# Sliding-window attention and an ELU layer on one core: which engine adds two kept products for a quarter of the output

## The chip, the core and the metric

The kernel runs on one core of a Trainium2 chip. A core has five engines that run their own instruction streams and meet through semaphores: TensorE (PE; its weight loads are listed as PEld), VectorE (DVE), ScalarE (ACT), GpSimd (POOL) and SyncE (SP), which here only issues transfers. The metric is the device time of one execution in microseconds, the median over runs of the same kernel. Lower is better.

## What is computed

The reference is attention with a sliding window and a linear distance bias, followed by two matrix products with an ELU between them:

```python
# q, k, v: (8, 8, 576, 64); w_in: (512, 2048); w_out: (2048, 512)
scores = scale * np.matmul(q, k.transpose(0, 1, 3, 2))
bias = slopes[:, None, None] * (-np.abs(rel))[None, :, :]
mask = (rel >= 0) & (rel < 128)
scores = np.where(mask, scores + bias[None], -1e9)
attn = softmax(scores)
x = np.matmul(attn, v).transpose(0, 2, 1, 3).reshape(4608, 512)
h = x @ w_in
g = np.where(h > 0.0, h, np.exp(np.minimum(h, 0.0)) - 1.0)
out = g @ w_out            # (4608, 512), float32
```

## The kernel before, in words

The 4608 tokens are cut into nine blocks of 512 (NTB = 9), and the attention runs over eight batches of 576 tokens. One hand-written schedule mixes three kinds of work in numbered slots (`s`): the attention of a later batch, the hidden layer of a token block (`hidden` and `elu`, into the tile `g`), and the output product of an earlier block. In each slot the loop at the end of the program issues first the `early` work, then the `hidden` products of the slot, the `elu` of the slot before, the slot's `tasks`, its output products (`OUT`), and the `late` work. The order in which the program calls things is the order in which each engine executes its own.

`hidden` (L305 to L316) multiplies on TensorE into one of the PSUM banks `hp`. ScalarE and GpSimd then make the exponential of the negative part in the SBUF tile `e`, in one of two ways. In slots named SOFT, ScalarE does both steps (L312, L313). In the others, two slots out of every eight, ScalarE takes the exponential (L315) and GpSimd clamps it (L316, called the clamp below). VectorE combines `e` and the bank into `g` (L323) and so frees the bank for a later hidden product.

The output product of most tokens is not computed with eight block products but with seven: for a pair `n` of output tiles (256 tokens, two tiles of 128 rows, `n` from 1 to 17) the 2048 rows of `w_out` and its 512 columns are halved, and sums of quarters are multiplied. Precomputed differences of `w_out` quarters stand in `T` (1 to 4), sums of `g` quarters are made on VectorE by `sums` into `S` (1 to 4, 128x1024 float16 each, L354). `product` (L393) runs the seven products, eight matmuls of 256 columns each, accumulating into two PSUM banks in turn (`op` and `av`). Products 1, 6, 7 and 5 are kept: ScalarE copies the bank into the SBUF tiles `U1`, `U6`, `U7`, `U5` (L396, 128x256 float32, one buffer each). The order of the products is 1, 2, 6, 5, 7, 3, 4, spread over eight slots, seven matmuls in each.

The four quarters of a pair's output are put together in `ob` tiles (three buffers): C11 = U1 + bank and C12 = U6 + bank on VectorE (`add`, L354), the lower left quarter as a plain copy of the bank by ScalarE (L398), and C22, the lower right quarter, as U7 + U5. C22 reads SBUF alone. It is called at the head of the tasks in the slot after the pair's last products, some 5 us after U7 was copied. After C12 and C22 the finished tile is stored by a transfer that SyncE issues (`put`, L412). The SyncE queue also carries the transposes of the attention's result into `xT`.

The last pair (n = 17) has a schedule of its own: all its products stand in two slots, and its C22 waits for the copies of products 5 and 7 shortly before the end.

Other work on VectorE in the same stretch: the multiplication of the exponentials with a table (`EX` by `TAB`, L241, 128x1024 float16, both in SBUF), the normalisation of the attention's result (`xn`, L260 and L277), and transposes of q and k from the staging tile `st` (L145). Other work on GpSimd: it issues the loads of q and k (`load_qk`, L108) and of v (`load_v`, L114), each issue a GpSimd instruction of 0.67 to 0.88 us.

Of the kernel before, what the change touches and what calls it, by code (L numbers as in the profile page):

```python
# [11 lines left out]
ALU = mybir.AluOpType  # L12
# [6 lines left out]
def kernel(  # L19
# [9 lines left out]
    nc = tc.nc  # L29
# [4 lines left out]
    NTB = NTOK // 512  # L34
# [3 lines left out]
    V = nc.vector  # L38
# [41 lines left out]
    op = ps_o.tile([128, 512], F32, name="op", tag="op")  # L80
# [68 lines left out]
    with tc.manual_schedule():  # L149
# [203 lines left out]
        def add(o, a, b, op=ALU.add):  # L353
            V.tensor_tensor(out=o, in0=a, in1=b, op=op)  # L354
# [16 lines left out]
        def place(n, i):  # L371


            z, x = XY[n] if n < 2 * NTB - 1 else (sp[2], sp[3] if i == 2 else sp[0])
            return (z if i in (1, 4, 6, 7) else x)[:, 0:256]

        def kept(n, i):
            if (n, i) not in U:
                U[n, i] = work.tile([128, 256], F32, name=f"U{i}", tag=f"U{i}", bufs=1)
            return U[n, i]  # L380

        def tile_out(n, i):
            if (n, i) not in obs:
                obs[n, i] = work.tile([128, DO], F32, name="ob", tag="ob")
            return obs[n, i]
# [14 lines left out]
        def combine(n, what):  # L400
            if what == "C11":
                add(tile_out(n, 0)[:, 0:256], kept(n, 1), place(n, 2))
            elif what == "C12":
                add(tile_out(n, 0)[:, 256:512], kept(n, 6), place(n, 3))
                put(n, 0, 0, DO)
            else:
                add(tile_out(n, 1)[:, 256:512], kept(n, 7), kept(n, 5))
                put(n, 1, 0 if n < 2 * NTB - 1 else 256, DO)

        def put(n, i, c0, c1, queue=nc.sync):  # L410
            r = 256 * n + 128 * i
            queue.dma_start(out[r:r + 128, c0:c1], tile_out(n, i)[:, c0:c1])  # L412
# [218 lines left out]
        for n in SEVEN:  # L631
            s = 15 + 8 * n
            ps = (19, 20, 21, 22, 23, 25, 27, 29, 30) if n == 1 else range(s, s + 9)
            if n < 2 * NTB - 1:
                for d, i in ((-1, 1), (1, 2), (3, 3), (4, 4)):
                    (at_once if n > 2 else at)(ps[d] if d > 0 else ps[0] - 1, sums, n, i)
                after(ps[2], combine, n, "C11")
                after(ps[6], combine, n, "C12")
                (at_once if n > 2 else at)(ps[8], combine, n, "C22")
                for d in range(8):  # L640
                    OUT[ps[d]] = [(product, (n, i, j, j + 1)) for i, j in turns[7 * d:7 * d + 7]]
            else:
                at_once(s - 3, sums, n, 3)
                for i in (2, 1):
                    at_once(s - 2, sums, n, i, 0, 6)
                    at_once(s - 1, sums, n, i, 6, 8)
                at(s - 1, product, n, 1)
                OUT[s] = [(product, (n, 2)), (combine, (n, "C11")), (sums, (n, 4)), (product, (n, 6)), (product, (n, 5))]
                OUT[s + 1] = [(product, (n, 7)), (product, (n, 3)), (combine, (n, "C22")), (combine, (n, "C12")),
                              (product, (n, 4)), (last_out, (n,))]  # L650
# [48 lines left out]
```

The softmax here doesn't subtract the row's maximum and nothing guards it: scores larger than these inputs give would overflow.

## Time and profile before

Three runs took 310.35, 310.82 and 310.94 us; the median is 310.82. One execution was profiled; its span from the first to the last instruction is 308.9 us.

| What | Value |
|---|---|
| median of three runs | 310.82 us |
| span of the profiled execution | 308.9 us |
| mean granted TensorE clock | 0.998 of full speed |
| VectorE sums U7 + U5 (`ob<-U,U`) | 17, mean 0.415 us, first at 70.3, last at 304.2 us |
| GpSimd clamps (`e<-e`, L316) | 44, median 0.612 us (0.602 to 0.838) |
| VectorE `EX` by `TAB` (L241) | 48, median 0.685 us |
| VectorE `S` sums of full size (L354) | 66, mean 0.68 us |
| stores from `ob` on SyncE | 35, landing after 2.2 us (median) |
| idle time of GpSimd before its clamps, until ScalarE's `e` | 152.9 us |

Busy time of each engine in stretches of the same execution, in us:

| Stretch (us) | PE | DVE | ACT | POOL |
|---|---|---|---|---|
| 70 to 90 | 19.9 | 18.9 | 17.0 | 8.8 |
| 90 to 120 | 29.9 | 27.5 | 25.4 | 10.7 |
| 150 to 180 | 29.9 | 27.3 | 25.2 | 9.9 |
| 240 to 270 | 29.9 | 25.0 | 26.3 | 1.8 |
| 270 to 290 | 20.0 | 15.0 | 15.1 | 1.2 |

In a line of the profile, L305 is line 305 of the program, `out<-in` are the tiles written and read, and the shapes are partitions x elements. In rows of the timeline the first number is the start in us from the beginning of the span, the second the length; a bracket at the end tells how long the engine had been idle and who ended it. A group's line gives total busy us and the mean of one in ns after the first bar, then the engine's idle time just before the group and what ended most of it. Two instructions of one engine can overlap slightly, since the next begins while the last results of the first are written.

### The profile page before, as it was taken

How to read it: one execution, taken by the hardware profiler on the slowest of the kernel's cores; microseconds unless marked ns; L12 is line 12 of the kernel's file. 1: busy time of each engine (PE TensorE's matmuls, PEld its weight loads, DVE VectorE, ACT ScalarE, POOL GpSimd, SP SyncE). 2: the span in 40 equal slices, each digit the busy share in tenths (PEclk: the TensorE clock that was granted, in tenths of full speed). 3: DMA queues.
4: the chain of work that ended last, by engine and by line, in shares of the span. 5: the costliest groups of instructions: out<-in, count | busy, mean ns of one | idle time of the engine just before them, and what ended most of it. 6: DMA issues, size and time to landing. Idle time of an engine off the chain costs nothing.

```text
span 308.9 us, 9820 instructions
## 1 busy us (share of the span) xinstructions
PE 300.1 (97%) x4071; PEld 256.1 (83%) x4071; DVE 257.5 (83%) x498; ACT 241.8 (78%) x446; POOL 108.4 (35%) x163
## 2 busy tenths in 40 slices
PE   6899999999999999999999999999999999999995
PEld 4788875798888888988888888888899888898884
DVE  4646888988989998997989998989998788886782
ACT  4576678678798788878887889778888897968871
POOL 8937867273252315141616061706000001010000
PEclk9999999999999999999999999999999999999999
DMA  9999999999194919395969896999530202030103
GB/s 96 196 197 202 201 180 185 94 118 115 21 165 63 169 35 161 43 152 59 132 70 138 110 102 78 138 124 122 60 94 7 91 17 87 19 98 0 70 28 110
DMA packets 96509, 32.04 MB, mean 104 GB/s; under 512 B 83920, under 2 KB 91984, under 8 KB 96464
## 3 DMA queue, kind: packets, MB, share of 16 engines
q0 software_dynamic: 75920, 18.36, 64.2%
q1 hardware_dynamic: 20400, 12.98, 17.1%
q8 instruction: 32, 0.52, 0.7%
q14 instruction: 13, 0.11, 0.1%
q10 hardware_dynamic: 144, 0.07, 0.1%
HBM read 36.70 MB, written 9.44 MB: 149 GB/s over the span
## 4 chain that ended last, share of the span: by engine, by line
PE 72%; DVE 8%; DMA 6%; ACT 5%; POOL 4%; issue 4%; POOLq 0%; DVEq 0%
PE hp L305 33%; PE op L393 13%; PE av L393 12%; DMA VP<-in_v_dram 4%; PE spa L225 3%; PE spa L271 3%; DVE g L323 3%; POOL e L316 2%; PE sp L393 2%; ACT e L315 2%; DMA s<-in_q_dram 2%; ACT EX L236 1%; PE sp L253 1%; POOL VP L114 1%; DVE xn L260 1%
## 5 line engine op out<-in xcount | busy, mean ns | idle before, releaser
L305 PE MATMUL hp<-xT,wi 128*128 128x256 f16 (+3 forms) x1488 | 144.2, 245 | 1.0 <-DVE g L323 0.5
L305 PEld LDWEIGHTS <-wi 128*128 128x128 f16 x1600 | 119.9, 98 | 18.1 <-issue 6.3
L323 DVE SCALAR_TENSOR_TENSOR g<-e,hp 128x512 f16<-128x512 f32 x138 | 93.7, 679 | 22.2 <-ACT e L313 12.5
L316 POOL TENSOR_SCALAR e<-e 128x512 f32<-128x512 f32 x44 | 28.0, 636 | 158.8 <-ACT e L315 152.9
L312 ACT ACTIVATE e<-hp 128x512 f32<-128x512 f32 x98 | 58.6, 597 | 28.5 <-PE hp L305 23.1
L313 ACT ACTIVATE e<-e 128x512 f32<-128x512 f32 x100 | 63.1, 631 | 3.2
L393 PEld LDWEIGHTS <-S 128*128 128x128 f16 x544 | 51.2, 98 | 6.7 <-issue 0.6
L393 PEld LDWEIGHTS <-g 128*128 128x128 f16 x408 | 38.2, 98 | 4.7 <-issue 0.6
L241 DVE TENSOR_TENSOR EX<-EX,TAB 128x1024 f16<-128x1024 f16 x48 | 32.9, 686 | 6.2 <-ACT EX L236 4.0
L114 POOL DMA_DIRECT2D VP<-in_v_dram x40 | 34.6, 878 | 0.6 <-PE hp L305 0.3
L315 ACT ACTIVATE e<-hp 128x512 f32<-128x512 f32 x40 | 24.1, 601 | 10.9 <-PE hp L305 10.9
L393 PE MATMUL op<-T,S 128*128 128x256 f16 x200 | 30.0, 273 | 0.1
L233 ACT ACTIVATE EX<-spa 128x1024 f16<-128x1024 f32 x24 | 24.6, 1025 | 3.7 <-PE spa L225 3.4
L393 PE MATMUL av<-T,S 128*128 128x256 f16 x176 | 26.4, 273 | 0.1
L236 ACT ACTIVATE EX<-sp 128x512 f16<-128x512 f32 x48 | 26.0, 596 | 0.0
L354 DVE TENSOR_TENSOR S<-g 128x1024 f16<-128x1024 f16 (+2 forms) x35 | 23.5, 671 | 0.8 <-PE op L393 0.2
L393 PE MATMUL op<-wo,g 128*128 128x256 f16 x128 | 19.2, 272 | 0.1
L393 PE MATMUL av<-wo,g 128*128 128x256 f16 x120 | 18.0, 272 | 0.0
L277 DVE TENSOR_TENSOR xn<-spa,rden 128x512 f16<-128x512 f32 x24 | 16.6, 692 | 0.8
L108 POOL DMA_DIRECT2D st<-in_k_dram x24 | 16.2, 686 | 2.8 <-DMA s<-in_q_dram 1.9
L108 POOL DMA_DIRECT2D st<-in_q_dram x24 | 15.9, 666 | 0.6 <-DMA VP<-in_v_dram 0.6
L271 PE MATMUL spa<-VP,EX 128*128 128x65 f16 x336 | 15.4, 193 | 0.1
(139 smaller groups left out, 379.3 us busy)
## 6 DMA issues: line engine op xcount, KB each, us to landing
out_dram<-ob SPq DMA_DIRECT2D x35, 256.0 KB, 2.2
VP<-in_v_dram POOLq DMA_DIRECT2D x32, 128.0 KB, 5.7
st<-in_k_dram POOLq DMA_DIRECT2D x24, 144.0 KB, 5.2
st<-in_q_dram POOLq DMA_DIRECT2D x24, 144.0 KB, 5.9
wi<-in_moe_w_in_dram POOLq DMA_DIRECT2D x4, 512.0 KB, 10.7
wo<-in_moe_w_out_dram POOLq DMA_DIRECT2D x4, 512.0 KB, 10.1
VP<-in_v_dram POOLq DMA_DIRECT2D x8, 64.0 KB, 5.8
s<-in_k_dram POOLq DMA_DIRECT2D x1, 512.0 KB, 12.1
```

The costliest lines, as they stand in the source:

```text
L108: nc.gpsimd.dma_start(st[b][32 * g:32 * g + 32, w, :, :, :, :].rearrange("p h n j d -> p (h n) (j d)"), (q, k)[w][b, 2 * g:2 * g + 2, :, : ...
L114: nc.gpsimd.dma_start(VP[b % 2][0:p, n, :, 0:D], v[b, :, 128 * n:128 * n + p, :].rearrange("h p d -> p h d"))
L236: nc.scalar.activation(unit(b, u)[:, g, :, :], sp[g].rearrange("p (h c) -> p h c", h=2), AF.Exp, scale=0.125)
L241: V.tensor_tensor(out=e, in0=e, in1=TAB[:, int(u == 3), 2 * gp:2 * gp + 2, :, :], op=ALU.mult)
L271: nc.tensor.matmul(a[:, h // 4, h % 4, :], ex_[u][:, c:c + 128], VP[b % 2][:, n, h, 0:D + 1], start=j == 0, stop=j == len(parts) - 1)
L305: nc.tensor.matmul(p[:, l * w + u0:l * w + u1], w_in_sb[:, c, fc * 128:(fc + 1) * 128], xT[:, c, x0:x0 + u1 - u0], start=(c == 0), stop=(c ...
L312: nc.scalar.activation(e[:, 0:n], p[:, 0:n], AF.Relu, scale=-1.0)
L313: nc.scalar.activation(e[:, 0:n], e[:, 0:n], AF.Exp, scale=-1.0)
L315: nc.scalar.activation(e[:, 0:n], p[:, 0:n], AF.Exp)
L316: nc.gpsimd.tensor_scalar(out=e[:, 0:n], in0=e[:, 0:n], scalar1=1.0, scalar2=0.0, op0=ALU.min, op1=ALU.max)
L323: V.scalar_tensor_tensor(out=gs[t][:, f0:f0 + nf, c0:c0 + w], in0=sh(es.pop((t, c0, f0))), scalar=1.0, in1=sh(hps.pop((t, c0, f0))), op0=A ...
L393: nc.tensor.matmul(o, a[:, j, :], b[:, j, :], start=j == 0 and i in (1, 2, 5), stop=j == 7, skip_group_check=True)
```

## The change

For the pairs 1 to 16 the sum U7 + U5 is issued to GpSimd in place of VectorE. Pair 17 keeps VectorE. The inputs, the output tile and the place in the program are the same.

```diff
             else:
-                add(tile_out(n, 1)[:, 256:512], kept(n, 7), kept(n, 5))
+                (V if n == 2 * NTB - 1 else nc.gpsimd).tensor_tensor(
+                    out=tile_out(n, 1)[:, 256:512], in0=kept(n, 7), in1=kept(n, 5), op=ALU.add)
                 put(n, 1, 0 if n < 2 * NTB - 1 else 256, DO)
```

In the instruction streams this takes 16 rows out of VectorE's and puts 16 into GpSimd's. There they stand as follows: one or two load issues after the last clamp of the pair for pairs 1 to 9, directly after the second clamp for pairs 10 to 14, and at the end of the queue for pairs 15 and 16. The order on TensorE, ScalarE and SyncE stays. ScalarE's copy into U5 of the next pair now also waits for GpSimd, and the store of the tile waits for ScalarE and GpSimd in place of ScalarE and VectorE.

## The prediction

> **What bounds the kernel now.** I read the page from the top: busy times, the chain that ended last, then the waits of TensorE, then single rows of the timeline around the sixteen sums that move.
>
> ```profile
> PE 300.1 (97%) x4071; PEld 256.1 (83%) x4071; DVE 257.5 (83%) x498; ACT 241.8 (78%) x446; POOL 108.4 (35%) x163
> ...
> PE 72%; DVE 8%; DMA 6%; ACT 5%; POOL 4%; issue 4%; POOLq 0%; DVEq 0%
> ```
> Two groups of instructions, each shape by itself (columns: line, engine, operation, tiles, shapes and count, then busy us and mean ns of one, then idle time before them and what ended it):
>
> ```profile
> L354 DVE TENSOR_TENSOR ob<-U,U 128x256 f32<-128x256 f32 x17 | 7.1, 415 | 1.9 <-ACT U L396 1.9
> ...
> L316 POOL TENSOR_SCALAR e<-e 128x512 f32<-128x512 f32 x44 | 28.0, 636 | 158.8 <-ACT e L315 152.9 <-issue 5.8
> ```
>
> TensorE (PE) is busy 300.1 of 308.9 us and most of its idle time lies before the first moved sum (70.25 us): over 69 to 300 us it is busy 230.2 of 231. VectorE (DVE) is full as well there, 203.8 of 231 us, but it is the second limit, not the first. The first group is the work that moves: 17 sums of two kept products, 0.415 us each, of which 16 go. The second is the only arithmetic that GpSimd (POOL) does in the steady part.
>
> A busy PE can hide short waits, since a row's modelled end reaches past the start of the next. So I took the starts of the single matmuls: a 256-column one normally follows its predecessor by 0.109 us (8 take 0.87). After 69 us, 26 starts are late by over 0.1 us, 4.4 us in all; before 25 of them a VectorE instruction had ended 0.05 to 0.06 us earlier. That 4.2 us is everything VectorE costs the path, and a ceiling for this change.
>
> **What is removed.** 16 x 0.415 = 6.6 us of VectorE time. It shortens the path only where the sum stands in an unbroken run of VectorE work that ends in a late matmul. I followed each of the 25 back to the first idle gap of VectorE. In 21 the run does not hold the sum: it starts at a wait for ScalarE or GpSimd, mostly a g that waits for its e. In four it does, at two places. The plainer is pair 3, in the VectorE rows and then the PE rows:
>
> ```profile
> 103.37 0.42 DVE L354 TENSOR_TENSOR ob<-U,U 128x256 f32<-128x256 f32 x1
> 103.70 0.17 DVE L259 RECIPROCAL rden<-sp 64x4 f32<-64x4 f32 x1
> ...
> 105.48 0.64 DVE L323 SCALAR_TENSOR_TENSOR g<-e,hp 128x512 f16<-128x512 f32 x1
> 106.05 0.66 DVE L354 TENSOR_TENSOR S<-S,g 128x1024 f16<-128x1024 f16 x1
> 106.65 0.76 DVE L145 STREAM_TRANSPOSE KT<-st 128x576 int32<-128x576 int32 x1
> 107.34 0.64 DVE L323 SCALAR_TENSOR_TENSOR g<-e,hp 128x512 f16<-128x512 f32 x1
> ```
> ```profile
> 106.17 1.03 PE L305 MATMUL hp<-xT,wi 128*128 128x256 f16 x8
> 107.04 0.38 PE L393 MATMUL av<-wo,g 128*128 128x256 f16 x2
> 107.26 0.71 PE L393 MATMUL op<-T,S 128*128 128x256 f16 x5
> 108.03 1.03 PE L305 MATMUL hp<-xT,wi 128*128 128x256 f16 x8
> ```
>
> The hidden products at 106.17 and 108.03 start just after a g has freed their bank, 0.19 and 0.23 us late; a third late start at 110.77 (0.10) ends the same run. Of the first, 0.09 is the change from 32-row to 128-row matmuls, which every such place shows and which stays. That leaves 0.10 + 0.23 + 0.10 = 0.43, and no more than the 0.415 by which the run moves up. Pair 1 gives 0.154 - 0.095 = 0.06 at 71.91. Sum of the gains: 0.47 us.
>
> The other 14 sums leave before a stretch in which VectorE waits for another engine anyway; their 5.8 us become idle time. At the end of the kernel (pair 16, sum at 300.91) the next products wait for PE itself: the S made at 301.58 is first used at 303.58.
>
> **What is added.** Sixteen sums on GpSimd, each 256 + 256 elements read and 256 written per partition. The trace of before has no two-input operation there. Nearest row: the clamp L316, 512 read and 512 written, 0.61 us when nothing disturbs it. Below: half of it, 0.31, if only the 256 outputs count. Above: twice, 1.22, if each input costs a pass of its own and the fixed part too. I take 0.65, near the row with equal reads.
>
> POOL has room: 108.4 us busy. What counts is where the sum stands in its queue. On VectorE it waited its turn, a slot or more after its inputs; on GpSimd it comes behind the second clamp of the pair, or behind one or two DMA issues after that. For pairs 1 to 14 the second kept product is done before then (pair 11: copied by 223.05, clamp over at 225.81), and for 15 and 16 the queue is empty and the sum starts when the copy ends. So nothing urgent waits behind it: the next clamp, which gates a g and so PE, is 11 to 14 us away. Behind the sums of pairs 1 to 10 stand one to five loads of q, k and v, each then some 0.65 us later, for a batch that is used many slots on; they land in 5 to 6 us by the page and nothing on the path waits for one after 70 us. On SP, the store behind the sum and the xT transposes behind that store see the sum at the old time or earlier. The U5 copy of the next pair on ScalarE now waits for GpSimd; it comes over 2 us after the sum (closest for pair 17, 302.91). Extra waits of some 0.02 us on ScalarE and VectorE I put at nothing, since both idle between groups; uncovered they would be 16 x 0.02 = 0.3.
>
> **What it may collide with.** GpSimd and VectorE get in each other's way in this trace: the clamp mostly takes 0.60 to 0.64 us, but the six that began 0.28 to 0.37 us before the end of a VectorE product of two SBUF tiles (EX by TAB) took 0.76 to 0.84. At 98.02 the clamp began while EX ran until 98.30, and ended 0.47 after it.
>
> ```profile
> 97.62 0.68 DVE L241 TENSOR_TENSOR EX<-EX,TAB 128x1024 f16<-128x1024 f16 x1
> ```
> ```profile
> 98.02 0.76 POOL L316 TENSOR_SCALAR e<-e 128x512 f32<-128x512 f32 x1 [8.62 <-ACT e L315]
> ```
>
> No row shows the reverse, a VectorE product that comes while GpSimd computes; by the rows a product could be held for nothing or for the whole sum. Places, from the GpSimd queue: pairs 1, 3, 4, 6, 7 and 8 ask while an S or EX is running and just wait (6 and 7 by only 0.08 and 0.03 us); pairs 2, 9, 14 and 15 meet nothing. In pairs 10 to 13 the sum starts as the clamp ends (225.81) and the next S comes at 226.57, then EX, then the values at 227.92, already late:
>
> ```profile
> 225.84 0.69 DVE L323 SCALAR_TENSOR_TENSOR g<-e,hp 128x512 f16<-128x512 f32 x1 [0.30 <-POOL e L316]
> 226.57 0.69 DVE L354 TENSOR_TENSOR S<-g 128x1024 f16<-128x1024 f16 x1
> 227.18 0.69 DVE L241 TENSOR_TENSOR EX<-EX,TAB 128x1024 f16<-128x1024 f16 x1
> ```
>
> The room is 0.76 us, so 0.65 passes and anything longer pushes PE by the excess. Pair 16's sum (299.95 to 300.60) may hold the S at 300.38 by 0.2, with 0.4 in hand. Pair 5 is the open one: the sum asks at 133.42, S runs until 133.59 and EX stands right behind it. If GpSimd gets in between, EX and the late values at 134.24 lose about 0.65 - 0.14 = 0.5 us (0.14 being the part of a clamp, 0.61 - 0.47, that passes before it is held). Cost 0 or 0.5; I take half, 0.25.
>
> The Trainium skill speaks against the change twice. "SBUF — State Buffer", Who interferes with whom: a VectorE instruction with two SBUF inputs and a GpSimd instruction that reads SBUF lock each other out, and the later one blocks fully. The 0.76 us clamps agree for one direction; no row here shows the other. "GPSIMD Engine Reference", Performance versus the Vector engine: a float32 add of 2048 columns takes 4497 ns; an eighth, 0.56 us, is my estimate from it, and with it the sum below would be about 0.05 us lower. No row here shows it.
>
> **Sum.** -0.47 + 0.25 = -0.2 us. The span would be 308.7; 1.9 us lie between the span of 308.9 and the median of 310.82, so 310.6. (The page gives no other time of the profiled execution.)
>
> **Rivals.**
> - *GpSimd's sum is long, and holds VectorE* (slower). At 1.22 us: S and EX of pairs 10 and 11 come 0.42 late with PE right behind (0.84), pairs 12 and 13 some 0.2 each behind a little slack, and pair 5 1.1. With the gain: -0.47 + 0.84 + 0.4 + 1.1 = +1.9, 312.7. It decides (over +0.6) from about 0.9 us on: 0.8 for pair 5 and 0.15 each for 10 to 12. For it: two operands through an engine that needs 0.61 for 512 elements of one. Against: equal reads in the nearest row, and the 0.415 saved soon after each hold.
> - *VectorE's room reaches PE everywhere* (faster). If a quarter of the 4.2 us of late starts goes, 1.05 us: 309.8. For it: VectorE above 90% from 70 to 120 us. Against: 21 of 25 runs hold no such sum and begin at a wait for ScalarE or GpSimd.
> - *Nothing reaches PE, either way*: 310.8, no different from the forecast by measurement.
>
> **How the numbers follow.** A measurement of this kernel tells no change from one within 0.2%, 0.62 us. The forecast with the third rival (310.2 to 311.4) gets 0.50, the long sum 0.34, the faster case 0.16. The range, 309.9 to 311.9, takes in pair 5 lost outright, sums up to about 1.0 us and some of the faster case.
>
> **What would show it.** The L354 sums on VectorE fall from 17 to 1 and a new GpSimd row of 16 appears at 0.6 to 0.75 us; VectorE busy falls by 6.6; the late starts at 106.17, 108.03 and 110.77 shrink together by 0.4. S after the clamp of pairs 10 to 13 still follows its g by 0.04 us: if it follows later, the rival is at work. EX at pair 5 directly after S, or half a microsecond later, settles that. Wrong makes it a GpSimd row above 0.9 us, or late starts that vanish where VectorE had waited for ScalarE.

## The result: 0.27% slower, and where it went

With the change the kernel takes 311.42 us (median of 16 runs, 310.88 to 313.49), against 310.80 us before (16 runs on the same chip, 309.85 to 311.43). The medians lie 0.62 us, 0.20%, apart. The ratio taken over the single runs, which all comparisons below use too, is 1.0027, with a 95% interval of 1.0016 to 1.0038: slower by 0.27%. That is small, near the 0.2% under which the prediction takes a change for none, but the interval lies above 1 altogether. The profiled execution has a span of 309.6 us, 0.7 us more than before.

The page of the changed kernel, busy times and the chain that ended last:

```profile
PE 300.1 (97%) x4071; PEld 255.9 (83%) x4071; DVE 254.6 (82%) x482; ACT 241.9 (78%) x446; POOL 122.2 (39%) x179
...
PE 75%; DVE 6%; ACT 6%; POOL 4%; DMA 4%; issue 3%; POOLq 0%; DVEq 0%; ACTq 0%
```

TensorE does the same work in the same busy time. VectorE has 16 instructions fewer, GpSimd 16 more. Three groups of the changed kernel, each shape by itself, with the columns of the groups shown before:

```profile
L241 DVE TENSOR_TENSOR EX<-EX,TAB 128x1024 f16<-128x1024 f16 x48 | 33.4, 697 | 7.3 <-ACT EX L236 4.6 <-ACT EX L233 2.6
L354 DVE TENSOR_TENSOR S<-g 128x1024 f16<-128x1024 f16 x33 | 23.7, 719 | 0.7 <-PE op L393 0.2
...
L407 POOL TENSOR_TENSOR ob<-U,U 128x256 f32<-128x256 f32 x16 | 14.2, 888 | 24.0 <-ACT U L396 23.9
```

The last line is the new one, mean 0.888 us. The first two are VectorE products that the change does not touch, and both are longer: S had a mean of 686 ns before (22.6 us in all), EX 686 (32.9). That is 1.1 + 0.5 us of VectorE time, though each of these instructions does the same work. A group mean can't say which ones; rows can. TensorE's waits, the view that names who was waited for, has a line that the kernel before does not have (total us, times, longest):

```profile
PE spa L271 <- DVE EX L241: 1.0, 2, 0.7
```

Two waits of TensorE for an EX, 0.26 and 0.74 us. They belong to pairs 4 and 5. These are the GpSimd (POOL), VectorE and TensorE rows at pair 5:

```profile
132.04 0.69 DVE L323 SCALAR_TENSOR_TENSOR g<-e,hp 128x512 f16<-128x512 f32 x1 [0.32 <-POOL e L316]
132.64 0.66 POOL L108 DMA_DIRECT2D st<-in_q_dram  x1
132.76 0.91 DVE L354 TENSOR_TENSOR S<-g 128x1024 f16<-128x1024 f16 x1
133.31 0.94 POOL L407 TENSOR_TENSOR ob<-U,U 128x256 f32<-128x256 f32 x1
133.60 1.21 DVE L241 TENSOR_TENSOR EX<-EX,TAB 128x1024 f16<-128x1024 f16 x1
...
134.86 0.42 PE L271 MATMUL spa<-VP,EX 128*128 128x65 f16 x8 [0.74 <-DVE EX L241]
```

The same place in the kernel before, where the sum was still on VectorE and came later:

```profile
132.89 0.69 DVE L354 TENSOR_TENSOR S<-g 128x1024 f16<-128x1024 f16 x1
133.50 0.69 DVE L241 TENSOR_TENSOR EX<-EX,TAB 128x1024 f16<-128x1024 f16 x1
...
133.84 0.82 PE L271 MATMUL spa<-VP,EX 128*128 128x65 f16 x16
```

Before, S and EX took 0.69 each here, and the values' product on TensorE ran through without an idle stretch. Now S takes 0.91 and EX 1.21, together 0.74 more, and TensorE stands for 0.74. The sum's row begins at 133.31, EX can begin only when S is through (133.60). EX ends at 134.81, which is 0.56 after the sum's end at 134.25. Pair 4, the same engines:

```profile
116.74 0.99 DVE L354 TENSOR_TENSOR S<-g 128x1024 f16<-128x1024 f16 x1
117.66 0.68 DVE L241 TENSOR_TENSOR EX<-EX,TAB 128x1024 f16<-128x1024 f16 x1
117.75 1.16 POOL L407 TENSOR_TENSOR ob<-U,U 128x256 f32<-128x256 f32 x1
...
118.39 0.42 PE L271 MATMUL spa<-VP,EX 128*128 128x65 f16 x8 [0.26 <-DVE EX L241]
```

Here EX is undisturbed and the sum waits for it (it ends 0.57 after EX). But S took 0.99, 0.30 too long, and it ended at 117.73, before the sum's row begins at 117.75. The row as the profile shows it can't be what held S; four of the experiments below ask what did.

The span also holds the loads at the start, which differ from those of the trace before by up to 0.8 us and once by 1.6. A sharper measure is the time of TensorE between the same two matmuls, from the one at 69.30 (time of the trace before) to the start of the last. It is called the TensorE interval below:

| Stretch (times of the trace before) | before | changed | difference |
|---|---|---|---|
| 69.30 to 110.77 (pairs 1 to 3) | 41.47 | 41.17 | -0.30 |
| 110.77 to 134.24 (pairs 4 and 5) | 23.48 | 24.54 | +1.06 |
| 134.24 to the last matmul | 170.98 | 171.07 | +0.09 |
| TensorE interval | 235.92 | 236.78 | +0.86 |

So there was a small gain where it was expected, and a loss of a microsecond in two pairs.

### The profile page after: what moved, and what is told of

Its sections match the earlier page's. It is cut to its first block, busy times and chain, and to the rows that moved or that the text cites. A ratio compares the mean times of both kernels' runs of the same rounds, so it can differ in the third digit from the quotient of the medians.

```text
span 309.6 us, 9854 instructions
## 1 busy us (share of the span) xinstructions
PE 300.1 (97%) x4071; PEld 255.9 (83%) x4071; DVE 254.6 (82%) x482; ACT 241.9 (78%) x446; POOL 122.2 (39%) x179
## 4 chain that ended last, share of the span: by engine, by line
PE 75%; DVE 6%; ACT 6%; POOL 4%; DMA 4%; issue 3%; POOLq 0%; DVEq 0%; ACTq 0%
PE hp L305 34%; PE op L393 13%; PE av L393 12%; PE spa L225 4%; DMA s<-in_q_dram 3%; PE spa L271 3%; DVE g L323 2%; PE sp L393 2%; ACT e L315 2%; POOL VP L114 2%; PE op L329 1%; POOL e L316 1%; PE sp L253 1%; DVE EX L241 1%; PE sp L305 1%
## 5 line engine op out<-in xcount | busy, mean ns | idle before, releaser
L354 DVE TENSOR_TENSOR S<-g 128x1024 f16<-128x1024 f16 (+2 forms) x35 | 24.8, 708 | 0.8 <-PE op L393 0.2
L407 POOL TENSOR_TENSOR ob<-U,U 128x256 f32<-128x256 f32 x16 | 14.2, 888 | 24.0 <-ACT U L396 23.9
```

## The experiments

Each kernel was timed beside the kernel before on its own chip; the TensorE interval is of its one profiled execution. The last two columns are the late starts of the values' product at pairs 4 and 5 (0.12 and 0.16 us before, 0.42 and 0.90 with the change).

| Run | us | before, us | ratio and interval | TensorE interval | pair 4 | pair 5 |
|---|---|---|---|---|---|---|
| e1_pairs45_on_vector | 310.58 | 310.81 | 0.9989 (0.9972 to 1.0006) | 235.93 | 0.13 | 0.16 |
| e2_only_pairs45 | 312.61 | 310.81 | 1.0048 (1.0030 to 1.0066) | 237.29 | 0.44 | 0.91 |
| e3_right_after_clamp | 310.21 | 310.81 | 0.9983 (0.9967 to 1.0000) | 235.69 | 0.12 | 0.16 |
| e4_gpsimd_writes_only | 310.81 | 310.81 | 1.0003 (0.9983 to 1.0024) | 235.68 | 0.12 | 0.16 |
| f1_pairs459_rows_0_31 | 312.37, one run | 311.14 | none | 237.30 | 0.12 | 0.71 |
| f2_pairs459_rows_64_127 | 311.00, one run | 311.14 | none | 235.76 | 0.12 | 0.09 |
| f3_wait_before_sum | 310.41 | 311.14 | 0.9976 (0.9954 to 0.9998) | 235.25 | 0.05 | 0.09 |
| f4_only_pairs13 | 311.05 | 311.14 | 0.9994 (0.9978 to 1.0011) | 236.25 | 0.12 | 0.16 |
| g1_pairs459_rows_0_63 | 312.35, one run | 310.84 | none | 237.12 | 0.44 | 0.90 |
| g2_clamp_then_wait_then_sum | 309.85 | 310.84 | 0.9979 (0.9960 to 0.9998) | 235.23 | 0.05 | 0.09 |
| g3_before_with_fills | 310.62 | 310.84 | 0.9998 (0.9978 to 1.0018) | 235.95 | 0.12 | 0.16 |
| h1_before_with_paired_fills | 310.55 | 310.63 | 0.9999 (0.9984 to 1.0013) | 235.51 | 0.05 | 0.08 |

### Are two sums the whole loss? (e1, e2)

One kernel gives the sums of pairs 4 and 5 back to VectorE, the other moves only these two:

```diff
-                (V if n == 2 * NTB - 1 else nc.gpsimd).tensor_tensor(
+                (V if n in (4, 5, 2 * NTB - 1) else nc.gpsimd).tensor_tensor(   # e1
+                (nc.gpsimd if n in (4, 5) else V).tensor_tensor(                # e2
```

> As changed, but the sums of pairs 4 and 5 go back to VectorE. Theory A (the loss is VectorE held by GpSimd's sum at these two places: late starts of 0.42 us at 118.39 and 0.90 at 134.86, where before had 0.12 and 0.16): the two late starts fall back to 0.1 to 0.2, the span to about 308.6, the ratio to the kernel before to about 0.9985. Rival B (many small costs: added waits on ScalarE and VectorE, loads issued 0.7 us later): two of sixteen sums less, so at most an eighth of the loss goes, ratio about 1.002.

> As before, but the sums of pairs 4 and 5 alone go to GpSimd. Theory A: the whole loss without the gain of pairs 1 and 3: late starts at pairs 4 and 5 longer by 0.3 and 0.75 us than before, ratio about 1.0033. Rival B: 2/16 of 0.8 us, ratio about 1.0003.

With fourteen sums on GpSimd and these two on VectorE, the stretch of pairs 4 and 5 takes 23.49 us, as before, and the kernel can't be told from the one before. (Pairs 1 to 3 take 41.15 in it, so the gain is there; two starts near 220 us, 0.16 and 0.09 late in this execution and in no other, use most of it up in its TensorE interval.) With these two alone on GpSimd the stretch takes 24.55 and the kernel is 0.48% slower; the stretch before it keeps its 41.47, so there is no gain to set against. One late start of 0.24 at 280.11 in e2's profile does not follow a VectorE instruction and is no part of the loss. The loss comes from two of the sixteen sums.

### Is it the place in GpSimd's queue? (e3)

The sum is split from the store and called right behind the pair's second clamp, ahead of the load issues (pairs 1 and 17 as they were):

```diff
-            else:
+            elif what == "add22":
                 (V if n == 2 * NTB - 1 else nc.gpsimd).tensor_tensor(
                     out=tile_out(n, 1)[:, 256:512], in0=kept(n, 7), in1=kept(n, 5), op=ALU.add)
+            else:
+                if n in (1, 2 * NTB - 1):
+                    combine(n, "add22")
                 put(n, 1, 0 if n < 2 * NTB - 1 else 256, DO)
...
                 after(ps[6], combine, n, "C12")
+                if n > 1:
+                    at_once(ps[6], combine, n, "add22")
```

> As changed, but for pairs 2 to 16 GpSimd's sum stands directly behind the second clamp of the pair, ahead of the load issues, as it already does for pairs 10 to 14. Theory A: the sum (0.73 us) runs beside the g that waits for the same clamp (0.04 + 0.69) and is over when the next S comes, so S and EX of pairs 4, 5 and 9 take 0.69 again; ratio about 0.9985. Rival C (any sum of two SBUF operands on GpSimd costs VectorE about its own length, wherever it stands): S behind the g is held at every pair, by up to 0.7 us, and the ratio stays at 1.003 or rises. Rival B: as the changed kernel, 1.0027.

Pair 5 of this kernel, GpSimd and VectorE:

```profile
131.40 0.73 POOL L407 TENSOR_TENSOR ob<-U,U 128x256 f32<-128x256 f32 x1
131.46 0.69 DVE L323 SCALAR_TENSOR_TENSOR g<-e,hp 128x512 f16<-128x512 f32 x1 [0.32 <-POOL e L316]
132.18 0.69 DVE L354 TENSOR_TENSOR S<-g 128x1024 f16<-128x1024 f16 x1
132.79 0.68 DVE L241 TENSOR_TENSOR EX<-EX,TAB 128x1024 f16<-128x1024 f16 x1
```

The same sum, moved past the load issues, runs in 0.73 us beside the g, which has one input in SBUF (`e`) and one in PSUM (`hp`). Neither delays the other, and S and EX have their 0.69 and 0.68 again. All sums of this kernel have a mean of 0.736 us. Pairs 1 to 3 take 41.15 (the gain stays), pairs 4 and 5 23.49 (the loss is gone), and the kernel comes out 0.17% faster than before, with an interval that just reaches 1.

### Reading or writing? (e4)

GpSimd fills the quarter with a constant in place of the sum for pairs 1 to 16; this quarter of the output is not computed.

```diff
-                (V if n == 2 * NTB - 1 else nc.gpsimd).tensor_tensor(
-                    out=tile_out(n, 1)[:, 256:512], in0=kept(n, 7), in1=kept(n, 5), op=ALU.add)
+                if n == 2 * NTB - 1:
+                    add(tile_out(n, 1)[:, 256:512], kept(n, 7), kept(n, 5))
+                else:
+                    nc.gpsimd.memset(tile_out(n, 1)[:, 256:512], 0.0)
```

> As changed, but GpSimd fills the quarter with zeros in place of adding U7 and U5 for pairs 1 to 16: the lower right quarter of these pairs is not computed. GpSimd still works at the same place of its queue but reads nothing. Theory A in its narrower form (VectorE's second SBUF operand and GpSimd's reading exclude each other): S and EX take 0.69 at all pairs, late starts at 4 and 5 at 0.1 to 0.2, ratio about 0.9985. Rival D (any GpSimd work holds VectorE): S or EX of pairs 4 and 5 are still stretched by the length of the fill, 0.2 to 0.4 us, ratio about 1.001.

Pair 5 of this kernel, the fill and the EX next to it:

```profile
133.91 0.33 POOL L410 MEMSET ob<- 128x256 f32 x1
134.00 0.69 DVE L241 TENSOR_TENSOR EX<-EX,TAB 128x1024 f16<-128x1024 f16 x1
```

The fill stands where the sum stood, it began 0.09 ahead of EX, and EX took its usual 0.69. So GpSimd's writing alone doesn't hold VectorE. What the sum has beyond the fill is its two reads, and its longer time; that it is the reads is the reading that fits, by exclusion. In time the kernel can't be told from before; in the trace its late starts at pairs 4 and 5 are those of before.

### What held S before the sum's row began? (f1, f2, g1)

At pair 4 S was long before the sum's row in the profile. One theory was that a part of GpSimd starts on the sum early, while another part still works at the load issues ahead of it. So the sums of pairs 4, 5 and 9 were cut by rows: GpSimd takes some rows, VectorE the rest, and VectorE all rows of the other pairs.

```diff
-                (V if n == 2 * NTB - 1 else nc.gpsimd).tensor_tensor(
-                    out=tile_out(n, 1)[:, 256:512], in0=kept(n, 7), in1=kept(n, 5), op=ALU.add)
+                rows = [(nc.gpsimd, 0, 32)] + [(V, p, q) for p, q in [(32, 64), (64, 128)]] if n in (4, 5, 9) else [(V, 0, 128)]
+                for eng, p, q in rows:
+                    eng.tensor_tensor(out=tile_out(n, 1)[p:q, 256:512], in0=kept(n, 7)[p:q, :], in1=kept(n, 5)[p:q, :], op=ALU.add)
```

That is f1; f2 gives GpSimd the rows 64 to 127, g1 the rows 0 to 63.

> As before, but for pairs 4, 5 and 9 GpSimd adds partitions 0 to 31 of the quarter and VectorE the other 96 (in two instructions). It asks what stretched S before the row of GpSimd's sum had even begun (S of pairs 4, 5 and 9: 0.99, 0.91 and 1.20 us, the sum's rows starting 0.02 us after the end of S, 0.36 before it and 0.49 before it). Theory E (the partitions whose GpSimd cores are not busy with a load issue start the sum early, the others when the issue is over; the early part holds S, the late part EX): with rows 0 to 31 alone, if those belong to the cores that issue loads, S takes 0.69 at all three pairs and EX at pair 5 is still held (about 1.2 us). Rival F (the sum works as one piece): S and EX are stretched as in the changed kernel.

> As before, but for pairs 4, 5 and 9 GpSimd adds partitions 64 to 127 and VectorE the first 64. Theory E: the mirror of the run with partitions 0 to 31: S is stretched (about 1.0, 0.9 and 1.2 us at pairs 4, 5 and 9) and EX at pair 5 takes 0.69, since no late part is left. Rival F: both stretched, or neither.

> As before, but for pairs 4, 5 and 9 GpSimd adds partitions 0 to 63 and VectorE the other 64. The run with partitions 64 to 127 did not decide: there the sum also waited for GpSimd's own semaphore, which this one and the run with 0 to 31 do not. Theory E (cores that issue no loads, here those of partitions 32 to 63, start the sum while the others still issue): S of pairs 4, 5 and 9 is stretched again, to about 1.0, 0.9 and 1.2 us, which partitions 0 to 31 alone did not do, and EX at pair 5 is held as well, by the late part (about 1.2 us). Rival F (S is stretched by something that only a full-height sum does): S takes 0.69 at all three.

Pair 5 of f1 (GpSimd has rows 0 to 31):

```profile
133.23 0.69 DVE L354 TENSOR_TENSOR S<-g 128x1024 f16<-128x1024 f16 x1
133.78 0.74 POOL L409 TENSOR_TENSOR ob<-U,U 32x256 f32<-32x256 f32 x1
133.84 1.24 DVE L241 TENSOR_TENSOR EX<-EX,TAB 128x1024 f16<-128x1024 f16 x1
```

Pair 5 of g1 (rows 0 to 63):

```profile
133.71 0.91 DVE L354 TENSOR_TENSOR S<-g 128x1024 f16<-128x1024 f16 x1
134.25 0.94 POOL L409 TENSOR_TENSOR ob<-U,U 64x256 f32<-64x256 f32 x1
134.53 1.21 DVE L241 TENSOR_TENSOR EX<-EX,TAB 128x1024 f16<-128x1024 f16 x1
```

With the rows 0 to 31 alone, S is never stretched (0.693, 0.691, 0.693 at pairs 4, 5 and 9), and only the hold that the row itself explains is left: the sum begins 0.06 ahead of EX, and EX takes 1.24. With 32 rows more, S is stretched again, 1.01 at pair 4 and 0.91 at pair 5, as with the whole tile. This points to the rows 32 to 63 (at least) as those whose work begins before the row in the profile, while the rows 0 to 31 begin with the row. At pair 9 g1 missed its expectation: nothing was stretched there. f2 missed too, S and EX stayed at their usual length everywhere, but it decides nothing on the rows 64 to 127: its sum also waited for a semaphore of GpSimd itself, which the sums of f1, g1 and the changed kernel do not, and such a wait alone has the same effect (next). The times of f1 and g1 hold extra VectorE sums and are not compared with the changed kernel's.

The traces also tell when the early part begins. Wherever the rows show an instruction of one engine held by one of the other, the held one ended some 0.56 to 0.59 us after its holder, and a sum takes 0.73 alone. So a sum that held S began about 1.30 us before S ended: at 100.60, 116.44, 132.38 and 195.81 in pairs 3, 4, 5 and 9 of the changed kernel. This is an estimate from these rows. The queue of GpSimd holds a separate wait of the sum (a record `EVENT_SEMAPHORE` of L407), which stands among the load issues ahead of it. It ends at 100.52, 116.36, 132.30 and 195.74, each time 0.07 to 0.08 before the estimate. It also accounts for pair 9 of g1: there this wait ended at 197.18, after S had begun at 197.07, so S came first. The estimate was made from the finished traces; no run varied the place of that wait.

### If the sum can't start early (f3, g2)

A fill of one column of the same tile, ahead of the sum on GpSimd, makes the sum wait for a semaphore of GpSimd itself, until the fill is done. f3 does this at the old place, g2 at e3's place.

```diff
+                if n < 2 * NTB - 1:
+                    nc.gpsimd.memset(tile_out(n, 1)[:, 256:257], 0.0)
                 (V if n == 2 * NTB - 1 else nc.gpsimd).tensor_tensor(
                     out=tile_out(n, 1)[:, 256:512], in0=kept(n, 7), in1=kept(n, 5), op=ALU.add)
```

> As changed, but GpSimd writes one column of the quarter first and the sum waits on its semaphore, so no core can begin the sum before all cores are done with what stands ahead. Theory E: S of pairs 4, 5 and 9 takes 0.69 again; the late start at pair 4 falls from 0.42 to about 0.12; at pair 5 the sum asks at about the time at which EX is handed over, so EX takes 0.69 or about 1.2. Ratio 0.9985 to 1.001. Rival F: as the changed kernel, 1.0027.

> Both mends together: the sum directly behind the second clamp for pairs 2 to 16, with the one-column fill ahead of it on whose semaphore it waits. In the run with the fill, the clamps no longer waited for GpSimd's own semaphore (1 of them, against 27 before), and began 0.09 us after ScalarE's e in place of 0.16. Theory H: those 0.07 us lie on the path where a g waits for its clamp (late starts at 146.97, 162.62, 212.44 and 227.92), so TensorE's time from 69.30 to its last matmul, 235.92 us before, is 235.2 to 235.4 as in the run with the fill. Without theory H it is 235.7 as in the run without it. But the fill delays the sum by about 0.15 us, so S of pairs 10 to 13 and of 3 to 5 and 8 and 9 may be held by 0.1. Ratio 0.997 to 0.999.

Pair 5 of f3:

```profile
133.41 0.69 DVE L241 TENSOR_TENSOR EX<-EX,TAB 128x1024 f16<-128x1024 f16 x1
133.53 1.15 POOL L409 TENSOR_TENSOR ob<-U,U 128x256 f32<-128x256 f32 x1
```

S was 0.69 long again (0.694, 0.692, 0.692 at pairs 4, 5 and 9), which is what the early start predicts. And since S was through earlier, EX came 0.12 ahead of the sum, and now the sum waited: 1.15 instead of 0.73, ending 0.58 after EX. Three kernels show the same rule at this place: the one that asks first goes on, and the other waits for it. In the changed kernel (sum 133.31, EX 133.60) and f1 (133.78, 133.84) EX lost; in f3 the sum did. In f2 the sum lost too, but the two rows (EX 133.91, sum 133.90) are too close to order.

f3 and g2 are the only two kernels whose interval lies below 1 altogether, if barely (0.9998 at the upper end): 0.24% and 0.21% faster than before. In g2 all sums take 0.72 to 0.73, and all S and EX of 1024 elements their usual length. Only the shorter S beside pair 16's sum, 128x768, takes 0.80, against 0.56 before. The changed kernel and g2 were each timed beside the kernel before, and their intervals (1.0016 to 1.0038 and 0.9960 to 0.9998) don't meet; so g2 beats the changed kernel too.

### The gain alone (f4)

```diff
-                (V if n == 2 * NTB - 1 else nc.gpsimd).tensor_tensor(
+                (nc.gpsimd if n in (1, 3) else V).tensor_tensor(
```

> As before, but only the sums of pairs 1 and 3 go to GpSimd: the gain without the loss. The step of the prediction that mattered for the gain says the late starts of TensorE at 71.91, 106.17, 108.03 and 110.77 shrink by 0.47 us together, ratio about 0.9985. Rival B (each sum that leaves VectorE gives the same small part): 2/16 of whatever the move brings, ratio 0.9995 or more, and the late start at 108.03 stays at 0.2.

Inconclusive. The late starts at 71.91, 106.17 and 108.03 fell to 0.09, 0.09 and 0.00, as in the changed kernel. But in this execution a ScalarE step began some 0.3 us late at 105.74, and two starts behind it were late by 0.19 and 0.21, so the stretch of pairs 1 to 3 took 41.54. In the six other executions in which the sums of 1 and 3 had moved (the changed kernel, e1, e3, e4, f3, g2) it took 41.14 to 41.20, against 41.47. What delayed ScalarE in f4 stays open.

### Why are f3 and g2 better than e3? (g3, h1)

Their TensorE interval is 0.4 us below e3's. In f3 the fills had a side effect: all but one of 27 clamps lost a wait for GpSimd's own semaphore and began 0.08 to 0.10 us after ScalarE's `e`, not 0.15 to 0.17. (In the trace of the changed kernel 30 separate waits stand at the clamp's line, in f3's 4.) The clamp gates a g, and the g frees TensorE's bank. To see whether this pays without any moved sum, fills were put into the kernel before, ahead of the VectorE sum; g3 has one to a sum (another column each), h1 two of the same column, the second waiting for the first:

```diff
+    spare = one([128, 32], F32, "spare")
...
             else:
+                nc.gpsimd.memset(spare[:, n:n + 1], 0.0)   # g3
+                nc.gpsimd.memset(spare[:, 0:1], 0.0)       # h1, twice
                 add(tile_out(n, 1)[:, 256:512], kept(n, 7), kept(n, 5))
```

> The kernel before, with all sums on VectorE, and one column of an unused tile filled by GpSimd beside each of them: nothing of the change, but the clamps lose their wait for GpSimd's own semaphore. Theory H: the clamps begin 0.09 us after ScalarE's e in place of 0.16, the late starts at 146.97, 162.62, 212.44 and 227.92 shrink by 0.07 each, and TensorE's time from 69.30 to its last matmul falls by 0.2 to 0.4 us from 235.92. Against it: that time stays at 235.9 and the better time of the run with the fill came from the sums.

> The kernel before, all sums on VectorE, with two fills of the same column of an unused tile by GpSimd beside each of them. The second waits for the first, and with that the clamps behind lose their wait for GpSimd's own semaphore (one left of 27), which the single fills of the run before did not bring about: there the clamps still began 0.15 to 0.16 us after ScalarE's e. Theory H: the clamps now begin 0.08 to 0.09 us after e, the late starts at 146.97, 162.62, 212.44 and 227.92 shrink by 0.07 each, and TensorE's time from 69.30 to its last matmul falls by 0.3 to 0.4 us from 235.92. Without theory H it stays at 235.9.

g3 tested nothing: against its expectation the clamps kept their wait (0.15 to 0.17). In h1 it is gone. A clamp of h1 (its lines stand one higher than before's) and the ScalarE step that it follows:

```profile
143.99 0.61 ACT L316 ACTIVATE e<-hp 128x512 f32<-128x512 f32 x1
...
144.68 0.62 POOL L317 TENSOR_SCALAR e<-e 128x512 f32<-128x512 f32 x1 [9.71 <-ACT e L316]
```

`e` ends at 144.60, the clamp starts 0.08 later. In the trace before the same `e` ended at 145.42 and its clamp began at 145.58, 0.16 later. The TensorE interval of h1 is 235.51, 0.41 below before's, in six steps of about 0.07 at 118.53, 134.24, 146.97, 162.62, 212.44 and 227.92, each behind a clamp and its g. f3 and g2 have the same six steps. So the traces show the saving at these places, and it is what sets these two apart from e3. The time of h1 does not resolve it: 0.9999 (0.9984 to 1.0013).

## Why the prediction was wrong

It forecast 310.6 us, no measurable change leaning to faster; it became 311.42, slower. By its own steps:

- **What the 6.6 us of VectorE are worth: right.** Nothing came of the fourteen sums that stand ahead of a VectorE wait. VectorE's busy time fell by 4.5 us in e3, where hardly anything is held: the rows overlap, so a removed row of 0.415 does not clear as much. With the change it fell by 2.9, since a held instruction counts as busy.
- **The gain at pairs 1 and 3: right in place, smaller in size.** 0.47 was forecast, 0.30 came. The starts at 71.91, 106.17 and 108.03 moved up by 0.06, 0.09 and 0.22, and small differences elsewhere in the stretch took back some 0.08. The one at 110.77 stayed at 0.12 late, so it did not end the same run, as the prediction held. The TensorE rows of the changed kernel at pair 3:

```profile
105.92 1.05 PE L305 MATMUL hp<-xT,wi 128*128 128x256 f16 x8
...
107.57 1.04 PE L305 MATMUL hp<-xT,wi 128*128 128x256 f16 x8
```

The two hidden products stand 1.65 apart, 1.86 before.

- **The sum's duration on GpSimd: right within its bounds.** 0.65 was taken, 0.725 to 0.73 is what an undisturbed one takes (pairs 10 to 14). The mean of 0.888 mixes these with waiting ones of up to 1.23. So the rival with a sum of 0.9 and more did not happen, though rows above 0.9 exist: they wait. The lower estimate of 0.56 that the prediction gave beside it was too short.
- **The room of 0.76 in pairs 10 to 13: right.** Pair 11 of the changed kernel: the sum is over 0.07 before S begins, and S still follows g (which ends at 227.22) by 0.04.

```profile
226.46 0.73 POOL L407 TENSOR_TENSOR ob<-U,U 128x256 f32<-128x256 f32 x1
226.53 0.69 DVE L323 SCALAR_TENSOR_TENSOR g<-e,hp 128x512 f16<-128x512 f32 x1 [0.30 <-POOL e L316]
227.26 0.69 DVE L354 TENSOR_TENSOR S<-g 128x1024 f16<-128x1024 f16 x1
```

- **Queues, loads, stores and added waits at nothing: right.** No late start of TensorE follows one of them. Pair 16's sum was misread: the copy that ends at 299.90 is one of pair 17, pair 16's own two end at 296.13 and 297.77, so the sum came earlier and met another S. This S, 128x768, took 0.22 more (0.78 for 0.56), the size that was forecast, and TensorE did not see it.
- **"What it may collide with": this step failed**, in three ways. It took the sum to ask for its operands when the load issues ahead of it end, at 133.42 for pair 5; the experiments point to a part of it that asks earlier, by 0.8 to 1.3 us in pairs 3, 4, 5 and 9 by the estimate above. First, pair 5 was costed at "0 or 0.5; I take half, 0.25". The hold of EX came, and at its price: EX lost 0.52, against 0.65 - 0.14 = 0.5 worked out. The half was wrong; what decides is who asks first, and by the prediction's own rows that was the sum, at 133.42, with EX still behind S until 133.59. Second, S in front of it was stretched by 0.22; the prediction had no such case, a sum that asks while an S runs was to "just wait". Third, by the same error pair 4 was counted as nothing and cost 0.30, all from its S. Pair 9, said to meet nothing, had its S stretched by 0.51 (to 1.20), and only some 0.02 of this reached TensorE.

The sum as measured: -0.30 (pairs 1 and 3) + 0.30 (pair 4) + 0.74 (pair 5) + 0.12 (the rest, small) = +0.86 on the TensorE interval, against -0.47 + 0.25. The start of the profiled execution was 0.15 shorter than before's, which leaves the 0.7 by which the span grew. By these terms the late EX of pair 5 alone, with neither S stretched, would give -0.30 + 0.52 + 0.12 = +0.34, below the 0.62 that can be told; the S of pairs 4 and 5, stretched ahead of the sum's row, bring the other 0.52. This split is worked out and no kernel has it alone; f1, where EX was held and no S stretched, comes near: its values' product at pair 5 started 0.71 late, against 0.90.

The prediction named a rule of the Trainium skill ("SBUF — State Buffer", Who interferes with whom) and said that no row showed its other direction. The runs show it now: a GpSimd sum that reads SBUF holds a VectorE product with two SBUF inputs (EX 1.21 and 1.24 for 0.69), its fill does not (e4, 0.69), and a g with one SBUF input neither holds nor is held (e3, 0.73 and 0.69). The page also says that "Issue order, not op shape, decides who blocks"; the changed kernel, f1 and f3 agree. Read by the rows alone, pair 4 does not: its S was issued first, at 116.74, and was stretched ahead of a sum whose row begins at 117.75. What reconciles the two stands on another page: "GPSIMD Engine Reference", Instruction dispatch, says that each of GpSimd's cores serves its own partitions and starts on the next instruction when it has done its share of the last. f1 and g1 agree with it for the rows 32 to 63.

## What to carry to other kernels

Before an operation on two SBUF tiles goes to GpSimd, look for each VectorE instruction with two SBUF inputs within about a microsecond on either side of it, and price both orders; an instruction in GpSimd's queue behind load issues can take effect before its row starts in the profile, here by 0.8 to 1.3 us as estimated. The safe place here was directly behind the GpSimd instruction whose result VectorE was waiting for, beside a VectorE instruction with one SBUF input: the same sixteen sums cost 0.27% at one place and took 0.17% off (interval up to 1.0000) at the other. And a saving on an engine that is not the bound is worth only what the late starts of the bounding engine trace back to it, here 0.30 of 6.6 us.

## What the runs showed of the hardware that was not expected

- Held instructions end 0.56 to 0.59 us after the one that held them, in both directions: the EX of pair 5 (0.56 after the sum), the sums of pairs 4 and 9 (0.57 after EX and S), f3's (0.58). That is less than their whole length, by some 0.13 for a VectorE product of 0.69 and about 0.15 for a sum of 0.73.
- A GpSimd instruction may begin on some rows before its start in the profile: S was stretched by 0.30, 0.22 and 0.51 at pairs 4, 5 and 9 behind load issues, not with the rows 0 to 31 alone, and not when the sum waits for a fill ahead of it. By the estimate above that part begins 0.07 to 0.08 us after the sum's own wait in the queue.
- The sum takes as long on 32 rows as on 128: 0.74 and 0.73 us.
- A wait of GpSimd for its own semaphore costs about 0.07 us on each clamp (starts at 0.15 to 0.17 and at 0.08 to 0.10 after `e`), and it can be taken away by an unrelated pair of one-column fills (h1).
